# Filler transposes kept to the first part, later landing estimates, and two tiles' diagonals moved to ScalarE

## Chip, cores and metric

One core of one Trainium2 chip. The metric is device time in microseconds for one launch. TensorE (PE), VectorE (DVE), ScalarE (ACT), GpSimd (POOL) and SyncE (SP) each run their own instruction stream in order; streams meet only through semaphores.

## The reference

Three stages follow one another on 3072 tokens (batch 4, sequence 768, 8 heads of 48):

```
for t in range(S):                      # attention: linear recurrence per batch and head
    cur = outer(u * k[t], v[t])
    y[t] = r[t] @ (state + cur)
    state = w * state + outer(k[t], v[t])
x  = y as 3072 x 384
h  = x @ w_in                           # 384 -> 2048
x2 = (h * sigmoid(h)) @ w_out           # 2048 -> 384
e  = argmax(x2 @ w_gate + bias[modality])       # one of 8 experts
out[token] = gate * (relu(x2[token] @ w1[e]) @ w2[e])   # 384 -> 1024 -> 384
```

## The kernel before

**Attention** is done in 24 chunks ("tiles") of 128 tokens, `attention(n)`. A tile's inputs come by two DMAs: `load_A` (r and k transposed, and v: 768 KB) and `load_B` (r and k as rows: 192 KB, or 384 KB from tile 9 on, `NZ = 9`). Three buffers (two `AB` and `stall`) take turns from tile 3 on. Then r and k are scaled by powers of w (L460 on DVE, L464 on POOL, L462 for the first three tiles), the scores are formed on PE (L487) and put by `copy_predicated` (L493, DVE) over a matrix whose diagonal holds the u term. That diagonal matrix is ident times a column, formed by ScalarE in eight `activation` calls (L475), except for the tiles in `DIAG_POOL = (1, 2)`, where GpSimd does it in two `tensor_tensor` calls (L469). PE then multiplies by v and by the state (L503), the result is split in two parts (L524, L527), and the state is updated (L544, L557, L559, L548).

**The first dense layer** runs over 8 blocks of 384 tokens and 16 slices of its hidden width (`moe1`): nine matmuls into `ph` (L618), SiLU and a split into a high and a low part (L622, L623, L625), nine matmuls into `pa` (L637). The weights of the 16 slices are loaded (L290) and split first (`convert`, L587 to L596). Blocks 0 and 1 are done in two halves; the second half is added to the first by DVE (L653). `route` follows a block: transposes (L686), logits (L697, L702), expert choice, and writing of the rows to DRAM (L764).

**The experts** are `expert(s)`, s from 0 to 8: gathers of rows (L915), weight splitting (L925, L929), matmuls (L949, L957), scaling (L961, L963) and scatter to the output (L966). Steps 0 to 7 take 384 tokens each, step 8 takes 128. A loop for tokens left over follows (L1078); each engine reads its count first (L1077), and all engines meet there.

**Order of the work.** All of this is first put into a list of operations, each with an engine, an estimated duration, a priority, dependencies and buffers to acquire and release. `Plan.order` runs these through a small event simulation in Python when the kernel is built: at each moment each engine takes the ready operation of the lowest priority number whose buffers are free. The start times that come out fix the order in which instructions are emitted. The plan's clock is not used on the chip; only the order stays. For an operation with `nbytes` the plan lets the bytes pass at 260 KB per us after those of earlier transfers, and adds 4.0 us until what depends on it may start. A load of tile n is ready for the plan when a buffer is free; the conditional DMA of L425 (it moves data only in a fallback for extreme decay rates) stands behind it on SP and waits for its landing.

**Fillers.** A hundred operations of priority 900 and up, each of four transposes of `ident` whose result nobody reads, acquire an `h` or an `a` bank. They come last in priority, so the plan places one wherever PE would have nothing else to do, at 0.45 us each:

```
    for i in range(100):
        add("PE", 0.45, 900 + i, lambda i=i: [pe.transpose(bank(("w", i))[:, 0:128], ident, ident) for _ in range(4)],
            acq=[("ha"[i % 2], ("w", i))], rel=[("w", i)], lat=0.0)
```

Fifty more such transposes (L305) stand at the very start, outside the plan.

Of the kernel before, what the change touches and what calls it, by code (L numbers as in the profile page):

```python
# [16 lines left out]
SP = mybir.EngineType.SP  # L17
# [21 lines left out]
VW = 128  # L39
AW = 8 * C + 4 * VW  # L40
TW = AW + 2 * DM
DIAG_POOL = (1, 2)
NZ = 9
ENGINES = ("PE", "ACT", "DVE", "POOL", "SP")
HALF = NFC // 2
# [11 lines left out]
class Plan:  # L57
# [7 lines left out]
    def add(self, eng, dur, prio, fn, deps=(), acq=(), rel=(), lat=0.2, nbytes=0):  # L65
        o = Op()
        o.eng, o.dur, o.prio, o.fn, o.lat, o.nbytes = eng, dur, prio, fn, lat, nbytes
        o.deps = [d for d in deps if d is not None]
        o.acq, o.rel = list(acq), list(rel)
        o.n, o.after, o.left = len(self.ops), [], 0  # L70
        self.ops.append(o)
        return o

    def order(self):
        for o in self.ops:
            o.left = len(o.deps)
            for d in o.deps:
                d.after.append(o)
        ready = {e: [] for e in ENGINES}
        busy = dict.fromkeys(ENGINES, 0.0)  # L80
        events, dma, t, done = [], 0.0, 0.0, []
        for o in self.ops:
            if not o.left:
                heapq.heappush(ready[o.eng], (o.prio, o.n, o))
        count = 0
        while True:
            moved = True
            while moved:
                moved = False
                for e in ENGINES:  # L90
                    if busy[e] > t + 1e-9 or not ready[e]:
                        continue
                    held, pick = [], None
                    while ready[e]:
                        x = heapq.heappop(ready[e])
                        need = {}
                        for p, _ in x[2].acq:
                            need[p] = need.get(p, 0) + 1
                        if all(len(self.free[p]) >= k for p, k in need.items()):
                            pick = x[2]  # L100
                            break
                        held.append(x)
                    for x in held:
                        heapq.heappush(ready[e], x)
                    if pick is None:
                        continue
                    o = pick
                    for p, key in o.acq:
                        self.slot[key] = (p, self.free[p].pop(0))
                    o.start = t  # L110
                    busy[e] = t + o.dur
                    end = t + o.dur + o.lat
                    if o.nbytes:
                        dma = max(dma, t + o.dur) + o.nbytes / 260e3
                        end = dma + 4.0
                    heapq.heappush(events, (busy[e], count, None))
                    heapq.heappush(events, (end, count + 1, o))
                    count += 2
                    done.append(o)
                    moved = True  # L120
            if not events:
                break
            t = events[0][0]
            while events and events[0][0] <= t + 1e-9:
                o = heapq.heappop(events)[2]
                if o is None:
                    continue
                for key in o.rel:
                    p, i = self.slot[key]
                    self.free[p].append(i)  # L130
                for a in o.after:
                    a.left -= 1
                    if not a.left:
                        heapq.heappush(ready[a.eng], (a.prio, a.n, a))
        assert len(done) == len(self.ops), (len(done), len(self.ops))
        self.span = t
        return sorted(done, key=lambda o: (o.start, o.n))


def moe_rwkv_kernel(tc, ins, out):  # L140
# [51 lines left out]
    tA = [t[:, 0:8 * C].rearrange("p (a q t) -> p a q t", a=2, q=4) for t in AB]  # L192
# [90 lines left out]
    def load_A(n, s):  # L283
        sp.dma_start(AB[s][:, 0:AW], ins["av"][n])

    def load_B(n, s, w_=0):
        sp.dma_start(AB[s][:, AW + w_ * DM:], ins["rk"][n * C:(n + 1) * C, w_ * DM:])
# [52 lines left out]
    for i in range(NP):  # L340
        n = 1 << i
# [12 lines left out]
    add = P.add  # L354
# [4 lines left out]
    def sl_(key):  # L359
        return P.slot[key][1]  # L360
# [5 lines left out]
    def gate(t):  # L366
        return add("POOL", 0.0, -99, lambda: None, lat=t)
# [3 lines left out]
# [3 lines that stand above are left out]
# [22 lines left out]
    def need_at(n):  # L396
        j, i = divmod(n, BT)
        gap = {0: 1.0, 1: 2.6, 2: 2.6}.get(j, NFC / BT)
        return FIRST[j] - 0.4 - (BT - 1 - i) * gap
# [8 lines left out]
    def attention(n):  # L408
        b, c = n % B, n // B
        j, i = divmod(n, BT)  # L410
        z = need_at(n)
        pp = ("tah", "htt", "att")[n] if n < 3 else "ttt"
        kA, kT = ("A", n), ("atb", n)
        if n < 3:
            P.slot[kA] = ("tA", n)
            if n < 2:
                P.free["tA"].remove(n)
            oA, oB = gate((0.1, 0.2, 2.2)[n]), add("SP", 0.5, -49 + n, lambda: load_B(n, n, 1), nbytes=200e3)
        else:
            oA = add("SP", 0.6, z - 9, lambda: load_A(n, sl_(kA)), acq=[("tA", kA)], nbytes=786e3)  # L420
            oB = add("SP", 0.6, z - 8.9, lambda: load_B(n, sl_(kA), int(n < NZ)), [oA], nbytes=393e3 if n >= NZ else 197e3)
        relA = [kA] if n != 2 else []

        def f_V():
# [40 lines left out]
        o_d = []  # L465
        if n in DIAG_POOL:
            for hf in range(2):
# [597 lines left out]
    for n in range(NTILE):  # L1065
        j = n // BT
        if n % BT == 0 and j >= 2:
            run_moe(max(i for i, x in enumerate(SEQ) if x[0] == j - 2) + 1)
        attention(n)
# [3 lines left out]
        expert(s)  # L1073
    with tc.manual_schedule():
        for o in P.order():
            o.fn()
    tn = nc.values_load(tailn, min_val=0, max_val=NMAX - NSTAT + NA + 1)  # L1077
    with tc.For_i(0, tn, 1) as i:  # L1078
        e_ids("t", lists[1], bass.ds(i + (NSTAT - 1 - NA), 1))
# [91 lines left out]
```

## Time and profile before

| | us |
|---|---|
| median of 3 runs | 808.32 (807.42 to 811.14) |
| the profiled execution | 806.15 |
| its span, first to last instruction | 804.4 |

The mean granted TensorE clock of the profiled execution is 0.995 of full speed. A view of the profile names instructions by engine and line; PE is the matmul itself, PEld the load of its weights, and an engine's name with a q its sequencer. Times are us from the start of the span unless marked ns.

### The profile page before, as it was taken

The page shows a single profiled execution, that of the slowest core. Times are in us where ns is not written, and L with a number is a line of the kernel's source. Part 1 is how long each engine was busy: PE and PEld are TensorE (multiplying, and loading weights), DVE is VectorE, ACT ScalarE, POOL GpSimd, SP SyncE. Part 2 cuts the span into 40 slices and gives each one's busy share as a digit, 9 for nine tenths or more (in the row PEclk, how much of TensorE's full clock was granted, in tenths as well). Part 3 has the DMA queues.
Part 4 walks back from the last instruction along what each step waited for, and adds up shares of the span by engine and source line. Part 5 has one row for each costly group of instructions (what it writes and reads, how often), then busy time and mean ns, then how long its engine had stood idle before and what let it go on. Part 6 is the DMA issues. An engine that isn't in the chain of part 4 may idle for free.

```text
span 804.4 us, 15749 instructions
## 1 busy us (share of the span) xinstructions
PE 791.2 (98%) x6348; PEld 760.0 (94%) x6348; DVE 425.7 (53%) x793; ACT 337.3 (42%) x726; POOL 227.9 (28%) x280
## 2 busy tenths in 40 slices
PE   8999999998999999999999999999999999999998
PEld 7998999987999999999999999999999999999998
DVE  7989965635534543644643522353866544654310
ACT  3566765443334334334334422364435434444200
POOL 5435302343423422522421203210432313220120
PEclk9999999998999999999999999999999999999999
DMA  6454433081511411411421024531675345500000
GB/s 245 153 177 184 167 119 108 28 79 44 90 59 59 91 60 60 89 60 61 85 65 59 11 22 180 224 120 68 217 217 187 128 135 199 196 28 1 30 35 2
DMA packets 23920, 83.27 MB, mean 104 GB/s; under 512 B 7659, under 2 KB 12152, under 8 KB 21538
## 3 DMA queue, kind: packets, MB, share of 16 engines
q1 hardware_dynamic: 19730, 72.55, 30.1%
q0 software_dynamic: 3968, 9.66, 3.6%
q8 instruction: 51, 0.84, 0.5%
q14 instruction: 27, 0.22, 0.2%
q10 hardware_dynamic: 144, 0.00, 0.0%
HBM read 78.92 MB, written 9.77 MB: 110 GB/s over the span
## 4 chain that ended last, share of the span: by engine, by line
PE 90%; DVE 4%; DMA 3%; issue 1%; ACT 1%; POOL 1%; DVEq 0%; POOLq 0%; SPq 0%; ACTq 0%
PE ph L618 24%; PE pa L637 23%; PE ph L949 13%; PE pa L957 12%; PE pt L503 4%; PE pa L372 3%; PE pt L487 3%; PE ph L372 2%; DMA xgb<-x_rows,it 2%; DMA AB<-in_av_dram 1%; PE pt L933 1%; PE ph L305 1%; PE pt L686 1%; PE pt L544 1%; PE pt L697 1%
## 5 line engine op out<-in xcount | busy, mean ns | idle before, releaser
L625 DVE TENSOR_TENSOR gl<-sg,gh 128x384 fp32r<-128x384 f32 x128 | 86.7, 677 | 136.4 <-ACT gh L623 135.9
L622 ACT ACTIVATE sg<-ph 128x384 f32<-128x384 f32 x128 | 63.0, 492 | 214.0 <-PE ph L618 205.6
L637 PE MATMUL pa<-Wh,gh 128*128 128x384 f32 x384 | 132.7, 346 | 0.0
L637 PE MATMUL pa<-Wh,gl 128*128 128x384 f32 x384 | 129.7, 338 | 0.5 <-DVE gl L625 0.4
L637 PE MATMUL pa<-Wl,gh 128*128 128x384 f32 x384 | 128.8, 335 | 0.0
L618 PE MATMUL ph<-xh,Wh 128*128 128x384 f32 x384 | 92.8, 349 | 0.0
L618 PE MATMUL ph<-xh,Wl 128*128 128x384 f32 x384 | 88.9, 339 | 0.1
L618 PE MATMUL ph<-xl,Wh 128*128 128x384 f32 x384 | 88.5, 338 | 0.0
L1034 ACT ACTIVATE gh<-ph 128x384 fp32r<-128x384 f32 (+1 forms) x66 | 32.7, 495 | 113.5 <-PE ph L949 112.9
L1036 DVE SCALAR_TENSOR_TENSOR gl<-ph,gh 128x384 fp32r<-128x384 f32 (+1 forms) x66 | 36.8, 558 | 81.1 <-ACT gh L1034 81.1
L637 PEld LDWEIGHTS pa<-Wh,gh 128*128 128x128 f32 x384 | 72.3, 188 | 3.2 <-issue 2.0
L637 PEld LDWEIGHTS pa<-Wh,gl 128*128 128x128 f32 x384 | 72.1, 188 | 1.2 <-DVE gl L625 1.2
L637 PEld LDWEIGHTS pa<-Wl,gh 128*128 128x128 f32 x384 | 72.3, 188 | 0.0
L618 PEld LDWEIGHTS ph<-xh,Wh 128*128 128x128 f32 x384 | 66.3, 189 | 4.8 <-issue 3.2
L966 POOL DMA_INDIRECT out_dram<-x2all,it x25 | 33.8, 1353 | 127.8 <-DVE x2all L963 114.6
L618 PEld LDWEIGHTS ph<-xh,Wl 128*128 128x128 f32 x384 | 69.3, 188 | 0.7 <-DVE Wl L596 0.7
L618 PEld LDWEIGHTS ph<-xl,Wh 128*128 128x128 f32 x384 | 69.5, 189 | 0.0
L929 DVE TENSOR_TENSOR Wl<-raw,Wh 128x1024 fp32r<-128x1024 f32 (+2 forms) x54 | 64.0, 1220 | 9.9 <-ACT Wh L925 9.9
L957 PE MATMUL pa<-Wh,gh 128*128 128x384 f32 x200 | 67.6, 338 | 0.8 <-DVE x2all L963 0.8
L957 PE MATMUL pa<-Wh,gl 128*128 128x384 f32 x200 | 67.5, 337 | 0.0
L957 PE MATMUL pa<-Wl,gh 128*128 128x384 f32 x200 | 67.0, 335 | 0.0
L475 ACT ACTIVATE atall<-ident,cs 128x128 f32<-128x128 f32 x176 | 57.2, 393 | 13.8 <-DVE cs L457 9.8
(226 smaller groups left out, 1385.2 us busy)
## 6 DMA issues: line engine op xcount, KB each, us to landing
raw<-in_we_dram SPq DMA_DIRECT2D x18, 1536.0 KB
AB<-in_av_dram SPq DMA_DIRECT2D x18, 768.0 KB
stall<-in_wio_dram SPq DMA_DIRECT2D x16, 768.0 KB
x_rows<-x2all SPq DMA_DIRECT2D x24, 192.5 KB
AB<-y_slow SPq DMA_DIRECT2D x16, 256.0 KB
stall<-in_av_dram SPq DMA_DIRECT2D x5, 768.0 KB
AB<-in_rk_dram SPq DMA_DIRECT2D x10, 384.0 KB
stall<-in_rk_dram SPq DMA_DIRECT2D x5, 384.0 KB
```

What stands on the lines that cost most here:

```text
L372: add("PE", 0.45, 900 + i, lambda i=i: [pe.transpose(bank(("w", i))[:, 0:128], ident, ident) for _ in range(4)], acq=[("ha"[i % 2], ("w", ...
L475: act.activation(atb[sl_(kT)][h % 2][:, h // 2, :], ident, AF.Copy, scale=cs[:, h:h + 1])
L618: pe.matmul(p, win(a, fc, kt), (xh, xl)[b_][j % 2][:, kt, :], start=i == 0, stop=i == len(ops) - 1)
L622: o_s = add("ACT", 0.5, s - 4, lambda: act.activation(sgb[sl_(kS)], hps[sl_(kH)][:, 0:n], AF.Silu), [o_g1], acq=[("sg", kS)])
L625: o_l = add("DVE", 0.55, s - 4, lambda: vv.tensor_tensor(glb[sl_(kG)][:, 0:n], sgb[sl_(kS)], ghb[sl_(kG)][:, 0:n].bitcast(F32), op=ALU.sub ...
L637: pe.matmul(a, g[:, ts], wout(wp_, fc), start=begin and i == 0, stop=end and i == 2)
L929: eng.tensor_tensor(e_view(buf, 1)[wi][sl], m2[s]["raw", wi][sl], e_view(buf, 0)[wi][sl].bitcast(F32), op=ALU.subtract)
L949: pe.matmul(p[:, i * n:(i + 1) * n], a[:, kt, fc * 128:(fc + 1) * 128], b_[xb][:, kt, 0:n], start=m == 0, stop=m == len(ops) - 1)
L957: pe.matmul(a[:, 0:DM], g[:, sl], wt_[:, fc, :], start=fc == 0 and m == 0, stop=fc == NFE - 1 and m == 2)
L966: i = gp.indirect_dma_start(out=out, out_offset=bass.IndirectOffsetOnAxis(ap=m2[s]["it"][:, t:t + 1], axis=0), in_=o, in_offset=None, boun ...
L1034: o2 = add("ACT", 0.62 if small else 0.5, z + k - 6, lambda kH=kH, kG=kG, m=m: act.activation(ghb[sl_(kG)][:, 0:m], hps[sl_(kH)][:, 0:m], ...
L1036: o3 = add("DVE", 0.7 if small else 0.57, z + k - 6, lambda kH=kH, kG=kG, m=m: vv.scalar_tensor_tensor(glb[sl_(kG)][:, 0:m], hps[sl_(kH)][ ...
```

## The change

Three edits. Fillers whose start on the plan's clock is 150 or later are not emitted (the plan still places them). For the loads of tiles 9 to 23 the plan expects the landing 7.8 us later (`load_A`) and 5.8 us later (`load_B`) than before; for every other transfer, 3.8 plus the default `lat` of 0.2 is the 4.0 of before. And no tile has its diagonal formed by GpSimd any more.

```diff
-DIAG_POOL = (1, 2)
+DIAG_POOL = ()
@@ Plan.order
                     if o.nbytes:
                         dma = max(dma, t + o.dur) + o.nbytes / 260e3
-                        end = dma + 4.0
+                        end = dma + 3.8 + o.lat
@@ attention
-            oA = add("SP", 0.6, z - 9, lambda: load_A(n, sl_(kA)), acq=[("tA", kA)], nbytes=786e3)
-            oB = add("SP", 0.6, z - 8.9, lambda: load_B(n, sl_(kA), int(n < NZ)), [oA], nbytes=393e3 if n >= NZ else 197e3)
+            oA = add("SP", 0.6, z - 9, lambda: load_A(n, sl_(kA)), acq=[("tA", kA)], nbytes=786e3, lat=8.0 if n >= NZ else 0.2)
+            oB = add("SP", 0.6, z - 8.9, lambda: load_B(n, sl_(kA), int(n < NZ)), [oA], nbytes=393e3 if n >= NZ else 197e3, lat=6.0 if n >= NZ else 0.2)
@@ the emission
         for o in P.order():
-            o.fn()
+            if o.prio < 900 or o.start < 150.0:
+                o.fn()
```

## Rows read from the trace of the kernel before

**Rows 1.** The page, part 1: busy time, share of span, instructions.
```profile
PE 791.2 (98%) x6348; PEld 760.0 (94%) x6348; DVE 425.7 (53%) x793; ACT 337.3 (42%) x726; POOL 227.9 (28%) x280
```

**Rows 2.** Busy time by stage, the filler line L372 alone (x is its count).
```profile
0.00:134.00 134.00, 23.35 (x180) 20.06 (x180) 1.00 0.46 163
134.00:772.50 638.50, 0.00 (x0) 0.00 (x0) 0.99 0.33 95
772.50:801.20 28.70, 24.50 (x220) 24.20 (x220) 1.00 0.07 24
```

**Rows 3.** The chain that ended last, 755 to 805: start, us, what.
```profile
772.96 1.31 PE ph L372 x12
...
776.36 0.44 PE pa L372 x4
776.79 2.09 PE pa L957 x12
778.89 8.30 PE pa L372 x76
```

**Rows 4.** Timeline at the end: start, us, engine, line, [idle before <-releaser].
```profile
772.47 0.58 ACT L961 ACTIVATE x2all<-pa,gt 128x384 f32<-128x384 f32 x1 [0.49 <-PE pa L957]
...
772.62 1.14 DVE L963 TENSOR_SCALAR x2all<-pa,gt 128x384 f32<-128x384 f32 x2
```

**Rows 5.** Line L1078 by engine: ns min/median/max, first and last start.
```profile
L1078 SPq EVENT_SEMAPHORE  x16: 17/28/16415, 696.4 to 799.6; - x16
...
L1078 PEldq EVENT_SEMAPHORE  x13: 51/51/51, 801.2 to 803.0; - x13
```

**Rows 6.** The chain that ended last, 130 to 200.
```profile
144.79 0.66 PE pt L686 x6
...
170.07 0.49 PE pt L544 x16
...
173.97 9.30 DMA AB<-in_av_dram
...
184.02 0.57 DVE x2all L653
...
184.63 1.54 PE pt L686 x6
186.18 2.88 PE ph L618 x9
```

**Rows 7.** Timeline of all engines, 183 to 185.
```profile
183.29 0.69 DVE L460 TENSOR_TENSOR AB<-AB,Pt 128x512 f32<-128x512 f32 x1 [6.72 <-DMA AB<-in_av_dram]
...
184.63 0.69 PE L686 MATMUL pt<-ident,x2all 128*128 128x128 f32 x2 [4.44 <-DVE x2all L653]
```

**Rows 8.** Busy us by 20 us: PE, PEld, DVE, ACT, POOL; clock, DMA.
```profile
180.00:200.00 20.00, 15.56 (x151) 14.05 (x151) 10.88 (x27) 6.59 (x18) 6.59 (x8) 0.83 0.11 45
...
500.00:520.00 20.00, 19.24 (x127) 18.41 (x126) 6.85 (x30) 7.35 (x19) 2.89 (x8) 1.00 0.69 281
```

**Rows 9.** Line L487 from 160 to 270: ns, first and last start.
```profile
L487 PE MATMUL pt<-stall x32: 272/272/373, 191.2 to 254.3; 48*128 48x128 f32 x32
```

**Rows 10.** SP's queue, 60 to 330: what waits for tile 12's landing.
```profile
204.95 0.09 SPq L425 DMA_DIRECT2D stall<-y_slow  x1
```

**Rows 11.** Timeline of ACT, POOL and DVE, 11 to 50.
```profile
13.58 2.45 ACT L475 ACTIVATE atall<-ident,cs 128x128 f32<-128x128 f32 x8 [4.47 <-DVE cs L457]
...
23.01 2.76 POOL L469 TENSOR_TENSOR atall<-ident,cs 128x512 f32<-128x512 f32 x2 [3.27 <-DVE cs L457]
...
17.04 1.79 DVE L592 SCALAR_TENSOR_TENSOR cx<-cx,stall 128x768 uint32<-128x768 uint32 x1
...
38.12 0.96 DVE L592 SCALAR_TENSOR_TENSOR cx<-cx,stall 128x768 uint32<-128x768 uint32 x1
```

**Rows 12.** The chain that ended last, 0 to 60.
```profile
31.78 0.44 PE ph L372 x4
32.21 1.60 PE ph L618 x9
```

## The prediction

> **What bounds the kernel now.** I read the page first: PE is busy for 791.2 of 804.4 us [rows 1], so the span is PE's instruction stream, and the question is only which part of that stream is work and where it still stands idle. The second view is the busy time of the filler line alone, by stage [rows 2]. The reader should see three numbers there: 180 transposes up to 134 us, none for the next 638 us, and 220 after 772.5 us. The fillers of the middle do not exist, because the plan found PE full there; those that were left over were placed at the end of the plan, after everything else. The third view is the chain at the end [rows 3] with the timeline of the other engines [rows 4]: the last real matmuls end at 778.9 us, and what the chain shows behind them is filler. The fourth, the semaphores of the closing loop [rows 5], shows what that costs: SP stood 16.4 us at one semaphore that ended at 799.6, while PE's own semaphores of that line begin at 801.2. So the other engines were through at about 783.2 and the span waited for fillers.
>
> The fifth view is the chain around 180 us [rows 6] and its timeline [rows 7], because a table by 20 us showed one stage where PE was busy for only 15.56 us, with a granted clock of 0.83 [rows 8]. There PE waited 4.44 us for DVE's L653, and DVE had stood 6.72 us in front of L460, the scaling of tile 11 (numbers of tiles follow from the order of the 24 loads), whose load landed only at 183.27 [rows 6]. L653 has nothing to do with tile 11; it stood behind L460 in DVE's stream.
>
> **The fillers at the end.** The edit removes those that the plan starts at 150 or later. The plan's clock and the chip's differ, but between the two groups lies an empty 638 us [rows 2], so a threshold anywhere in it removes the 220 and keeps the 180. What PE's end sets after that: the engines meet at 783.2 instead of 799.6, which is 16.4 us. To this comes what the fillers between the last real matmuls cost: 1.31 us at 772.96 and 0.44 us at 776.36 [rows 3]. The second comes back whole. The first only in part, since the matmuls behind it need an accumulator that ACT and DVE were emptying: ACT's scaling ends at 773.05, DVE's two at 773.76 [rows 4]. The fillers ended at 774.27, so 0.5 to 1.2 us come back. I take 0.8, as the plan gives out the bank that came free first, less a little for the hand-over. Together 1.2 us, bounds 0.9 and 1.6. Last, what follows the meeting: it took 4.8 us (799.6 to 804.4), but PE's semaphores of L1078 began only at 801.2, when its fillers were through, so up to 1.6 us of this belong to the fillers too; the rest may be PE's own branch. Half of it is 0.8. Sum: 16.4 + 1.2 + 0.8 = 18.4 us, bounds 17.3 (16.4 + 0.9) and 19.6 (16.4 + 1.6 + 1.6).
>
> Without fillers PE stands idle for up to a us at 773. A pause of 0.76 us in the stage from 500 to 520 left the clock at 1.00, and the pause of 4.44 us was the one after which it fell [rows 7, 8]; the new pause is nearest to the short one, so I cost it at nothing. The Trainium skill, "TensorE: Matmul & The Clock Gate", section "HAM oscillation — how this bites in real kernels", speaks against taking fillers away: a PE that pauses between bursts of matmuls goes back to the lower clock. By it the end would be as under "clock" below; the two pauses of this trace leave that a small chance.
>
> **Landings expected later.** This edit adds no instruction and no transfer; it moves places in the streams. For tile 11 the plan's clock starts where the last reader of the buffer, L544, ends: 170.07 + 0.49 = 170.56 [rows 6]. Before, it expected the landing 0.6 + 786/260 + 4.0 = 7.6 us later, that is at 178.2; the real one came 12.7 us later, since SP issued the load only at 173.97 and it then took 9.30 us. DVE was there at 183.29 - 6.72 = 176.6 and stood. With the edit the plan expects 15.4 us, or 186.0, which is later than the real landing. L653's input came from matmuls that ended before 180.19 (184.63 - 4.44, where PE ran dry), so in the plan L653 goes ahead of L460, and PE goes on at once. What comes back: 4.44 us of idle time, and the lower clock after it. L618's nine matmuls took 2.88 us there [rows 6] and 1.60 elsewhere [rows 12], six transposes 1.54 instead of 0.66 [rows 6]: 2.2 us. Sum 6.6 us. If another stall takes its place, or this one stays, nothing: the bounds are 0 and 6.6.
>
> What is moved behind each load is L460 on DVE, L464 and the products of r, k and u on POOL, and L425 on SP, which waits for the landing. SP and POOL gain: what stands behind these in their streams, the row stores of L764 and the state scaling of L548, no longer waits for a load. None of the moved work is close to its need: tile 12 had landed at 204.95 [rows 10], and its scores are the last of the L487 row, at 253 to 254 [rows 9]. 7.8 us out of 48 are hidden by that distance.
>
> **The diagonals of tiles 1 and 2.** Four GpSimd instructions go, 16 ScalarE instructions come. One tile's eight took 2.45 us on ScalarE, GpSimd's pair 2.76 [rows 11], so the step itself shortens by 0.3 us for a tile; but the first of the two mask copies needed only GpSimd's first half, and now needs seven of eight activations. Behind the 16 on ScalarE stand L587 and L595 of the weight conversion and L524 of the tile before. From above: if all of it falls on the path to the first dense matmuls, 2 x 2.45 = 4.9 us slower. From below: DVE gets faster, because L592 took 1.79 us beside GpSimd's pair and 0.96 without [rows 11]; three such instructions at 0.83 give 2.5 us. The first real L618 came right behind fillers [rows 12], so in this stage PE's stream does not wait for DVE; the plan's own gaps, filled, set the time. DVE's relief does not enter the plan, and on the plan's clock eight activations cost 2.56 us against 2.8 for the pair. I take 0.
>
> The Trainium skill, "GPSIMD Engine Reference", section "8. Key points", says that GpSimd shares its SBUF interfaces with VectorE and that the two contend when VectorE reads two SBUF inputs. L592 has two such inputs, and the trace agrees (1.79 against 0.96 us). By that rule alone the first part would shorten; it is the "relief" below.
>
> **Sum.** 18.4 + 6.6 + 0 = 25.0 us. Against the profiled execution: span 804.4 - 25.0 = 779.4, its own time 806.15 - 25.0 = 781.2. The median of the runs shown lies 2.2 us above that execution, so 808.3 - 25.0 = 783.3, which I predict.
>
> **Rivals.** *Stall stays or moves*, 0.18: the plan's new order puts another DVE instruction in front of PE's next input, or tile 11's load is later still because more stores now go ahead of it on SP. For it: the real lag of 12.7 us is only 2.7 below the new estimate. Against it: with DVE moved, only a load later by that much does harm. 808.3 - 18.4 = 789.9. *ScalarE late*, 0.10: the 16 activations hold up conversion; PE's count of fillers before 134 us would grow. 783.3 + 4.9 = 788.2. *Relief*, 0.08: 783.3 - 2.5 = 780.8. *Clock*, 0.04: the pause at 773 lets the clock fall for the last two groups of matmuls, which took 2.09 us each [rows 3]; 783.3 + 4.2 = 787.5. *Starved*, slower than before, 0.02: the later landings push a tile's scores past their need, and PE, whose gaps no longer get fillers after 150, stands idle. There are 15 such tiles; up to 7.8 us each would give 783.3 + 117 = 900, and it outweighs the gain from 1.7 us a tile (25.0 / 15). It decides only if the distance of 48 us is used up, which nothing in the rows does. My forecast has 0.58.
>
> **How the numbers follow.** Low end: the upper bound of the end (1.2 more) and relief (2.5 more) give 779.6; the profiled execution's place under the median takes 2.1 off that, 777.5. High end: the stall case, 789.9, with a little of the lower bound of the end, 790.5. Relief, ScalarE and clock lie within. A difference of 0.5% (4 us) is about what a measurement of this kernel can tell from none. All cases but the last are faster by far more; for several small losses together I leave 0.02 within 0.5%. So faster 0.96, same 0.02, slower 0.02.
>
> **What would show it.** The filler line has about 180 transposes, all before some 140 us, and none at the end; the engines meet within 2 us of the last scatter's landing. No stage after 20 us has a clock under 1.00, and DVE's L460 has no long wait for a DMA. L475 counts 192, L469 is gone, L592 has no 1.79 any more, and the first L618 of the chain stands within 2 us of 32.2. The prediction is wrong if the clock falls in some stage between 140 and 770, if the count of early fillers changes by more than 20 transposes, or if the meeting at the end waits for something other than PE.

## The result, and the profile after

The changed kernel took 781.89 us (median of four runs, 780.16 to 783.08) against 809.73 for the kernel before in the same rounds; the ratio is 0.9652, with a 95% interval from 0.961 to 0.9693. The forecast was 783.3 in a range from 777.5 to 790.5. The profiled execution's span fell from 804.4 to 778.4 us, by 26.0 where the sum said 25.0; the two medians lie 27.8 us apart. One execution of the changed kernel in a later round (e11) took 1912.51 us, for a reason that no trace here shows, and is left out of every median and ratio below.

To see where it went I cut both spans at the same pieces of PE's work: the first dense matmul (L618), the first transposes of `route` (L686), the matmuls of tile 9 (the tenth group of L503, as tiles count from 0), and the last expert matmul (L957). These times are the starts of PE's instructions in the traces, the last one an end. The third row holds the stall at 180 us. The first two rows do not hold the same work on both sides, as shown under "The first part".

| us | before | after | difference |
|---|---|---|---|
| start to the first L618 | 32.0 | 33.1 | +1.1 |
| to the first L686 | 110.8 | 110.7 | -0.1 |
| to tile 9's L503 | 52.2 | 45.3 | -6.9 |
| to the end of the last L957 | 584.0 | 582.0 | -2.0 |
| to the end of the span | 25.5 | 7.4 | -18.1 |

**The end.** PE has 28 us less to do than in [rows 1], and the filler line has no instruction after 140 us, where [rows 2] had 220. The page's first part, then the filler line by stage (PE, PEld, clock, DMA):

```profile
PE 763.3 (98%) x6104; PEld 733.9 (94%) x6104; DVE 400.1 (51%) x793; ACT 341.8 (44%) x742; POOL 214.1 (28%) x276
```

```profile
0.00:140.00 140.00, 19.52 (x156) 17.36 (x156) 0.98 0.47 164
140.00:770.00 630.00, 0.00 (x0) 0.00 (x0) 1.00 0.30 95
770.00:778.00 8.00, 0.00 (x0) 0.00 (x0) 0.88 0.15 52
```

The closing loop's semaphores answer to [rows 5] (the line is now L1079). Under them stand SP's waits that end in the last 18 us (us in total, times, longest); the longest began far ahead of that window:

```profile
L1079 SPq EVENT_SEMAPHORE  x16: 17/28/892, 690.0 to 775.1; - x16
...
L1079 PEldq EVENT_SEMAPHORE  x13: 51/51/1100, 771.1 to 775.5; - x13
```

```profile
SPq L1079 <- DMA out_dram<-x2all,it: 83.8, 2, 82.9
```

PE's first semaphore of that line now begins at 771.1, right behind its last matmul, and SP's last one at 775.1. What SP waits for is the last scatter's landing and no longer PE. From the meeting to the end of the span it is 3.3 us (775.1 to 778.4), where it was 4.8.

**The stage at 180.** Busy time by stretch (PE, PEld, DVE, ACT, POOL, clock, DMA), for [rows 8] and two more; then PE's and DVE's timeline, for [rows 6, 7]:

```profile
40.00:60.00 20.00, 18.02 (x151) 16.85 (x151) 13.96 (x19) 12.12 (x29) 3.62 (x3) 0.83 0.35 122
180.00:200.00 20.00, 20.00 (x200) 18.38 (x199) 12.01 (x34) 8.33 (x23) 8.81 (x12) 1.00 0.39 120
...
766.00:771.00 5.00, 4.85 (x27) 4.28 (x25) 1.28 (x3) 0.58 (x1) 3.15 (x6) 1.00 0.21 79
```

```profile
180.51 0.69 PE L618 MATMUL ph<-xl,Wh 128*128 128x384 f32 x3
181.04 0.90 PE L686 MATMUL pt<-ident,x2all 128*128 128x128 f32 x6
```

```profile
180.32 1.49 DVE L653 TENSOR_TENSOR x2all<-pa,x2all 128x384 f32<-128x384 f32 x3
...
187.81 1.21 DVE L460 TENSOR_TENSOR AB<-AB,Pt 128x512 f32<-128x512 f32 x1
```

L653 now stands ahead of tile 11's L460, PE has no idle time in the stage, and its clock is 1.00.

**The first part.** PE's order changed here. The state matmuls (L544) of three tiles stood behind the first L618 before (first fence) and stand ahead of it now (second fence), with four transposes more; behind the first L618 there are 60 transposes of L372 instead of 88. PE is busy for 28.76 us up to the first L618 before and for 29.84 after, and idle for 3.2 us in both.

```profile
31.97 0.78 PE L618 MATMUL ph<-xh,Wh 128*128 128x384 f32 x3
...
33.74 0.56 PE L544 MATMUL ph<-AB 128*48 128x48 f32 x16
```

```profile
28.98 0.56 PE L544 MATMUL ph<-AB 128*48 128x48 f32 x16
...
30.88 0.53 PE L544 MATMUL pt<-x2all 128*48 128x48 f32 x16
...
33.06 0.78 PE L618 MATMUL ph<-xh,Wh 128*128 128x384 f32 x3
```

The row from 40 to 60 is new: 18.02 us busy, clock 0.83, where the kernel before has 19.92 and 1.00. PE's timeline shows a pause of 1.56 us, and six us from 46 on at 0.50 of full speed, which is 1.2 GHz (the window stands under it):

```profile
41.22 0.95 PE L454 MATMUL pt<-ub,zb 128*128 128x2 f32 x8
43.73 1.16 PE L487 MATMUL pt<-AB 48*128 48x128 f32 x16 [1.56 <-issue]
```

```profile
46.00:52.00 6.00, 6.00 (x21) 6.00 (x21) 3.27 (x6) 4.36 (x11) 1.00 (x1) 0.50 0.02 7
```

DVE and GpSimd at the same time, for [rows 11]:

```profile
16.74 0.95 DVE L592 SCALAR_TENSOR_TENSOR cx<-cx,stall 128x768 uint32<-128x768 uint32 x1
...
36.30 1.92 DVE L592 SCALAR_TENSOR_TENSOR cx<-cx,stall 128x768 uint32<-128x768 uint32 x1
38.14 1.64 DVE L625 TENSOR_TENSOR gl<-sg,gh 128x384 fp32r<-128x384 f32 x1
39.70 2.05 DVE L594 CUSTOM_DVE_ANT_0 cx<-stall,cx 128x1536 uint16<-128x1536 uint16 x1
...
42.95 0.68 DVE L460 TENSOR_TENSOR AB<-AB,Pt 128x512 f32<-128x512 f32 x1
```

```profile
35.92 1.48 POOL L464 TENSOR_TENSOR AB<-AB,Qt 128x512 f32<-128x512 f32 x1
...
39.44 1.50 POOL L464 TENSOR_TENSOR AB<-AB,Qt 128x512 f32<-128x512 f32 x1
40.90 1.71 POOL L480 TENSOR_TENSOR AB<-AB,PKt 128x384 f32<-128x384 f32 x1
```

Tile 3's L460 ends at 43.63, and PE goes on with tile 3's scores (L487) at 43.73. L592 took 0.95 us where GpSimd's diagonals had stood beside it (16.74), but 1.92 beside GpSimd's scaling of tiles 3 and 4. ScalarE has the 16 added activations, 192 in all:

```profile
L475 ACT ACTIVATE atall<-ident,cs 128x128 f32<-128x128 f32 x192 | 62.0, 397 | 18.9 <-DVE cs L457 10.5 <-DMA x2all<-y_slow 4.3 <-DVE cs L440 3.9
```

### The profile page after: what moved, and what is told of

Read it like the earlier page. It is cut to its first block, busy times and chain, and to the rows that moved or that the text cites. A ratio compares the mean times of both kernels' runs of the same rounds, so it can differ in the third digit from the quotient of the medians.

```text
span 778.4 us, 15275 instructions
## 1 busy us (share of the span) xinstructions
PE 763.3 (98%) x6104; PEld 733.9 (94%) x6104; DVE 400.1 (51%) x793; ACT 341.8 (44%) x742; POOL 214.1 (28%) x276
## 5 line engine op out<-in xcount | busy, mean ns | idle before, releaser
L625 DVE TENSOR_TENSOR gl<-sg,gh 128x384 fp32r<-128x384 f32 x128 | 81.0, 633 | 154.5 <-ACT gh L623 146.6
L618 PE MATMUL ph<-xh,Wh 128*128 128x384 f32 x384 | 92.9, 350 | 0.0
L618 PE MATMUL ph<-xh,Wl 128*128 128x384 f32 x384 | 88.8, 339 | 0.0
L618 PE MATMUL ph<-xl,Wh 128*128 128x384 f32 x384 | 88.5, 338 | 0.0
L618 PEld LDWEIGHTS ph<-xh,Wh 128*128 128x128 f32 x384 | 66.2, 189 | 4.4 <-issue 3.0
L475 ACT ACTIVATE atall<-ident,cs 128x128 f32<-128x128 f32 x192 | 62.0, 397 | 18.9 <-DVE cs L457 10.5
L618 PEld LDWEIGHTS ph<-xl,Wh 128*128 128x128 f32 x384 | 69.5, 189 | 0.0
L618 PEld LDWEIGHTS ph<-xh,Wl 128*128 128x128 f32 x384 | 69.5, 188 | 0.0
L957 PE MATMUL pa<-Wh,gh 128*128 128x384 f32 x200 | 67.5, 337 | 1.0 <-DVE x2all L963 0.8
L957 PE MATMUL pa<-Wh,gl 128*128 128x384 f32 x200 | 67.4, 337 | 0.0
L957 PE MATMUL pa<-Wl,gh 128*128 128x384 f32 x200 | 67.0, 335 | 0.0
```

The source lines that it names most:

```text
L475: act.activation(atb[sl_(kT)][h % 2][:, h // 2, :], ident, AF.Copy, scale=cs[:, h:h + 1])
L618: pe.matmul(p, win(a, fc, kt), (xh, xl)[b_][j % 2][:, kt, :], start=i == 0, stop=i == len(ops) - 1)
L625: o_l = add("DVE", 0.55, s - 4, lambda: vv.tensor_tensor(glb[sl_(kG)][:, 0:n], sgb[sl_(kS)], ghb[sl_(kG)][:, 0:n].bitcast(F32), op=ALU.sub ...
L957: pe.matmul(a[:, 0:DM], g[:, sl], wt_[:, fc, :], start=fc == 0 and m == 0, stop=fc == NFE - 1 and m == 2)
```

## The experiments

There were twelve runs. The cuts of the table above, for the profiled execution of each:

| kernel | to first L618 | to first L686 | to tile 9's L503 | to last L957 | to end | span |
|---|---|---|---|---|---|---|
| before | 32.0 | 110.8 | 52.2 | 584.0 | 25.5 | 804.4 |
| after | 33.1 | 110.7 | 45.3 | 582.0 | 7.4 | 778.4 |
| after, again (e11) | 33.4 | 109.1 | 47.0 | 581.8 | 7.7 | 778.9 |
| e1, fillers alone | 31.3 | 110.9 | 52.2 | 582.6 | 7.4 | 784.3 |
| e2, landings alone | 31.0 | 111.2 | 48.5 | 586.2 | 25.5 | 802.5 |
| e3, diagonals alone | 33.3 | 108.7 | 51.0 | 585.3 | 28.1 | 806.4 |
| e4, e1 with e2 | 31.1 | 110.5 | 47.2 | 585.0 | 7.5 | 781.3 |
| e5, landing of tile 11 alone | 34.8 | 111.1 | 45.4 | 584.2 | 25.5 | 800.9 |
| e6, after with a bridge | 33.1 | 107.4 | 45.3 | 582.0 | 7.3 | 775.2 |
| the bridge again (e12) | 32.5 | 107.4 | 49.2 | 583.3 | 7.3 | 779.7 |
| e7, after with no filler | 32.4 | 114.2 | 45.4 | 584.1 | 7.3 | 783.5 |
| e8, e4 with 3 for 4 | 30.9 | 110.1 | 45.3 | 582.4 | 7.4 | 776.1 |
| e9, after, GpSimd relieved | 36.6 | 105.9 | 47.7 | 583.8 | 7.7 | 781.6 |
| e10, e6 with 3 for 4 | 34.1 | 108.6 | 47.3 | 583.1 | 7.7 | 780.9 |

### Fillers alone (e1)

```diff
         for o in P.order():
-            o.fn()
+            if o.prio < 900 or o.start < 150.0:
+                o.fn()
```

> Only the fillers after 150 are left out; landings and diagonals as in the kernel before. Theory (the end waits for PE alone): the streams are the same up to 772 us, so the span falls by what the two ends differ in, 19.5 us (1.3 between the last matmuls, 18.2 behind them), to about 785; PE's 4.44 us stall and the lower clock between 180 and 190 stay. Rival (the other engines' own closing work sets the end and only part comes back): 12 us or less.

Median 789.97, ratio 0.9769 (0.9729 to 0.9808), span 784.3, 20.1 us shorter. Behind the last L957 it is 7.4 us instead of 25.5, and tile 9 to the last L957 is 1.4 shorter. The stall at 180 is untouched:

```profile
184.83 1.54 PE L686 MATMUL pt<-ident,x2all 128*128 128x128 f32 x6 [4.43 <-DVE x2all L653]
```

### Landings alone (e2), and that of tile 11 alone (e5)

```diff
-                        end = dma + 4.0
+                        end = dma + 3.8 + o.lat
```

with `lat=8.0` and `6.0` for tiles 9 to 23 in e2, and for `n == 11` alone in e5.

> Only the landing estimates are changed; all 400 fillers and GpSimd's diagonals stay. Theory (one DVE instruction in front of another block's drain): the first 140 us are as before, the stall at 180 us goes with the lower clock after it, span shorter by 6.9 us, to about 797.5, with 220 fillers at the end. Rival (a stall moves elsewhere, the gain seen in the full change comes from its other first part): span within 2 us of before.

Median 804.72, ratio 0.994 (0.9905 to 0.9975), span 802.5: 1.9 us shorter, where 6.9 was expected (by the ratio, over ten executions, it is 4.9 us). The stall is gone, but the stage has a new pause, and another stands at 405, both in the middle of a group of matmuls that waits for no semaphore:

```profile
178.36 0.69 PE L618 MATMUL ph<-xh,Wl 128*128 128x384 f32 x3 [2.91 <-issue]
...
406.90 0.57 PE L503 MATMUL pt<-atall,AB 128*32 128x128 f32 x5 [1.69 <-issue]
```

> The kernel before with the later landing for tile 11 alone (all 220 late fillers stay). Theory: the landing term is one load's. The stall of 4.42 to 4.44 us at 180 and the low clock behind it go, the stage from the first L686 to tile 9's L503 shortens by 3.7 (as in the run with all landings) to 6.9 us (as in the changed kernel), and the span goes from 804.4 to 797.5 to 800.7. Rival: the later landings of the other 14 tiles carry part of it, then the stage shortens by less than 2 us. Second rival: the order shifts where PE's code comes in, and a pause in the middle of a group of matmuls takes 1.5 to 3 us of it back at some other place.

Median 799.77, ratio 0.9898 (0.9847 to 0.9949). The stage takes 45.4 us instead of 52.2: the whole gain, from one load. Its span shows only 3.5 of it, since this execution came to its first L618 2.8 us later than the one of before, with the same instructions up to there: the clock was 0.50 from 16 to 22 us, where before has 1.00, and PE had not been idle from 10 to 15.5 us. DVE's timeline, the stage and that stretch:

```profile
180.80 1.60 DVE L653 TENSOR_TENSOR x2all<-pa,x2all 128x384 f32<-128x384 f32 x3 [1.54 <-PE pa L637]
...
188.32 0.69 DVE L460 TENSOR_TENSOR AB<-AB,Pt 128x512 f32<-128x512 f32 x1
```

```profile
180.00:200.00 20.00, 20.00 (x201) 18.45 (x200) 10.80 (x32) 7.95 (x21) 3.46 (x7) 1.00 0.37 87
...
16.00:22.00 6.00, 6.00 (x41) 5.22 (x42) 6.00 (x9) 1.07 (x2) 3.14 (x2) 0.50 0.55 172
```

So the term is tile 11's alone; the later landings of the other 14 tiles brought nothing that shows.

### Diagonals alone (e3), and the other two edits without them (e4)

```diff
-DIAG_POOL = (1, 2)
+DIAG_POOL = ()
```

> Only the diagonals of tiles 1 and 2 go to ScalarE. Theory (this edit alone changes the first part): 156 fillers before 134 us, a pause of 1.5 to 2 us near 43 us with a lower clock to about 52 us, and the first transposes of L686 about 1 us later than before; span 1 us longer at that place (804 to 807 in all, as the stall at 180 us may shift). Rival (the first part's change comes from the landing estimates): 180 fillers, nothing at 43 us.

Median 809.08, ratio 1.0011 (0.998 to 1.0042): no difference. The table shows what cancels. The first L618 comes 1.3 us later, behind the three L544 and the four transposes more that the changed kernel has there too. The plan finds 24 fewer places for early transposes in all (156 instead of 180, as after the change), 28 fewer of them behind the first L618, and the stretch up to the first L686 is 2.1 us shorter. In this kernel the 24 reappear at the end, which is 2.6 us longer (28.1 against 25.5). The stage at 180 is 1.2 us shorter and what follows 1.3 longer. The pause at 43 is here too, with the clock at 0.91 from 40 to 60, so it belongs to this edit:

```profile
43.58 1.16 PE L487 MATMUL pt<-AB 48*128 48x128 f32 x16 [1.19 <-POOL AB L480]
```

> The full change without its diagonals: GpSimd keeps tiles 1 and 2. Theory (the diagonals cost 1.0 us net): span about 777.4, 1 us shorter than with the full change, 180 early fillers, no lower clock between 40 and 60 us. Rival (ScalarE's diagonals pay): span above 779.

Median 783.53, ratio 0.9694 (0.9626 to 0.9763), span 781.3. The gains of e1 and of the stall add up, less two pauses at the places of e2:

```profile
176.37 0.68 PE L618 MATMUL ph<-xh,Wl 128*128 128x384 f32 x3 [1.56 <-issue]
...
404.90 0.52 PE L503 MATMUL pt<-atall,AB 128*32 128x128 f32 x6 [1.68 <-issue]
```

Since the whole change has neither pause, it looked at this point as if the diagonals' edit paid 2.9 us by shifting PE's code. The next runs were to test that.

### PE's code shifted (e8)

```diff
-        ... lambda i=i: [pe.transpose(bank(("w", i))[:, 0:128], ident, ident) for _ in range(4)],
+        ... lambda i=i: [pe.transpose(bank(("w", i))[:, 0:128], ident, ident) for _ in range(3)],
```

> Fillers and landings edited, diagonals as before (profiled span 781.3), with three transposes for each early filler in place of four. PE's instruction stream gets some 90 instructions shorter ahead of 140 us, so that the 16 KB pieces of its code (256 instructions) are fetched some 8 us later against the work around them. Theory (the pauses of 1.56 us at 174.8 and 1.67 us at 403.2 come from a slow fetch of PE's code behind tile's index lists' small scatters): both pauses go or move to another group, the stage from the first L686 to tile 9's L503 is 1.5 us shorter (45.7 instead of 47.2), and the span 777 to 780 if the first part stays. Rival (the pauses belong to these groups of matmuls, whatever the fetch): both stay at the same groups and the span changes by less than 1 us. The first part shows besides whether a filler costs PE time: up to 4.9 us earlier if so, 0 if not.

Median 779.44, ratio 0.9654 (0.9611 to 0.9697), span 776.1. Both pauses were gone and the stage took 45.3 us, as the theory said; fillers a quarter shorter gave 0.4 us in the first part. But the fetch that the theory blames was there as before. Of q8, which fetches one 16 KB packet of code at a time, here is the one packet in e2 from 169 to 176 us, and in e8 from 163 to 170; 3.1 and 3.2% of 16 engines over 7 us are 3.5 and 3.6 us, where most such packets took 0.9 to 1.3. Only e2 paused behind it:

```profile
q8 instruction: 1, 0.02, 3.1%
```

```profile
q8 instruction: 1, 0.02, 3.2%
```

### The bridge (e6), the control (e11) and the bridge again (e12)

```diff
         def f_sc(qs):
+            if n == 3:
+                for _ in range(14):
+                    pe.transpose(bank(("sc", n, 0))[:, 0:128], ident, ident)
             for q in qs:
```

> The changed kernel with 14 more transposes into the score bank right ahead of tile 3's scores, where PE paused for 1.56 us at 42.2 to 43.7 and after which the granted clock was 0.50 from about 45 to 52.5. Theory: the pause is what let the clock fall. With it bridged the window from 40 to 60 has a clock of 0.97 or more instead of 0.83, the first L686 comes 2 to 3.5 us earlier (140.3 to 141.8 instead of 143.75), and the span is 775 to 776.5 instead of 778.4. Rival: the clock fell for another reason, such as the narrow matmuls ahead of the pause; then the low stretch stays and the span is 778.4 to 780.

Median 777.54, ratio 0.9638 (0.9599 to 0.9677), span 775.2. The stretch to the first L686 is 3.3 us shorter than after, and the clock in the window is 1.00, with the eight narrow matmuls (L454) still there. (Lines behind L482 count three more here: L485 is the bridge, L490 the scores.)

```profile
41.29 0.95 PE L454 MATMUL pt<-ub,zb 128*128 128x2 f32 x8
42.10 1.73 PE L485 MATMUL pt<-ident 128*128 128x128 f32 x14
43.76 0.49 PE L490 MATMUL pt<-AB 48*128 48x128 f32 x4
```

```profile
40.00:60.00 20.00, 19.64 (x190) 18.36 (x189) 16.64 (x24) 14.75 (x34) 4.06 (x3) 1.00 0.47 157
```

Three us lie within the intervals of runs made apart, so the changed kernel and the bridge ran once more in the same rounds.

> The changed kernel itself once more, as a control on the same chip and in the same rounds as the kernel with the bridge, since 3 us lie within the intervals of runs made apart. Theory: PE's pause ahead of tile 3's scores belongs to this instruction stream and comes again (1 to 1.6 us near 42), with a granted clock under 0.95 in 40 to 60; the span is 778 to 781. Rival: it was an accident of one execution, then the clock there is 1.00 and the span 775 to 776.5.

Ratio 0.9685 (0.9657 to 0.9712), median 781.27, span 778.9. The pause is back at the same scores, the clock of the window is 0.91:

```profile
44.03 1.16 PE L487 MATMUL pt<-AB 48*128 48x128 f32 x16 [1.57 <-POOL AB L480]
```

> The changed kernel with the bridge once more, beside the control. Theory: no pause near 42, clock 0.97 or more in 40 to 60, and a median 2 to 3.5 us under that of the control in the same rounds. Rival: the 3.2 us between the two profiled spans were scatter from one execution to the next; then the two medians differ by less than 1 us.

Ratio 0.9674 (0.9644 to 0.9704), median 781.14. At its place the bridge did what it did before: no pause near 42, clock 1.00, and a stretch of 107.4 us, as in e6. But the median is only 0.1 us under the control's, so the rival's number came out, though the mean clock of an execution is 0.994 to 0.998 here and 0.990 to 0.994 in the control. What takes the clock's gain back can be seen in the one profiled execution alone. The profiled span is 779.7, 4.5 us above that of the very same kernel in e6, because two pauses now stand where e2 and e4 had them, the first with a clock of 0.50 behind it (178 to 180.5):

```profile
40.00:60.00 20.00, 19.63 (x190) 18.35 (x189) 16.61 (x25) 15.42 (x34) 2.97 (x3) 1.00 0.48 169
```

```profile
176.17 0.42 PE L621 MATMUL ph<-xl,Wh 128*128 128x384 f32 x1 [2.08 <-issue]
...
405.31 0.33 PE L640 MATMUL pa<-Wl,gh 128*128 128x384 f32 x1 [1.33 <-issue]
```

This takes the shifted code down as an explanation: one instruction stream has the pauses in one execution and not in the other. Nor is a slow fetch needed, as the first of the two shows. Around the pause at 174 to 176 the queues of this execution moved only a tile's loads from 172.5 to 176.2, and q8's one packet from 161 to 175 took 0.4% of 16 engines over 14 us, or 0.9 us:

```profile
q8 instruction: 1, 0.02, 0.4%
```

### No fillers at all (e7)

```diff
-            if o.prio < 900 or o.start < 150.0:
+            if o.prio < 900:
```

> The changed kernel with the 156 early transposes of L372 left out too. Theory A (they fill gaps that PE has anyway and hold the clock): without them the first part has stages at the granted clock of 0.50 and lower means, the first L686 comes at 146 or later instead of 143.75, and the span is 781 to 790. Theory B (they stand in PE's way): each four take 0.45 us or less of PE's time, 156 of them at most 17 us, the clock stays at 1.00 in most stages, and the span is 765 to 777.

Median 781.92, ratio 0.9673 (0.962 to 0.9727), span 783.5. Theory A: the stretch to the first L686 is 3.5 us longer, with pauses of 3.04 us at 25 and 1.60 at 43, and the clock well down:

```profile
20.00:40.00 20.00, 15.30 (x161) 12.36 (x153) 17.52 (x20) 14.54 (x31) 8.37 (x6) 0.68 0.63 208
40.00:60.00 20.00, 17.98 (x141) 16.82 (x142) 14.44 (x20) 11.10 (x25) 4.16 (x3) 0.74 0.29 97
```

The early fillers' 19.5 us of PE time cost nothing that shows and hold the clock, but what they hold is worth some 3 us of one span, and the ratio cannot tell it from the changed kernel's.

### GpSimd relieved (e9)

```diff
-            o_k = add("POOL", 1.4, z - 3.2, lambda: gp.tensor_tensor(*scale(1), op=ALU.mult), zd)
+            o_k = add("POOL", 1.4, z - 3.2, lambda: gp.tensor_tensor(*[x[:, 0:1] if n in (3, 4) else x for x in scale(1)], op=ALU.mult), zd)
```

and the same cut for `nat(1), nat(1), PKt` of these two tiles.

> The changed kernel, same order on every engine, but GpSimd's scaling of k for tiles 3 and 4 (two L464 of 128x512) and its product for the state there (two L480 of 128x384) work on a part only (128x128 and 128x48), so the output of these tiles lacks the rest. Theory: DVE is slow between 34.5 and 43 us because GpSimd works beside it (L592 1.92 us instead of 0.96, L594 2.05 instead of 0.96), and that makes PE pause at 42.2. With some 4 us less of GpSimd's work there, DVE reaches tile 3's L460 by 41.5 or earlier instead of 42.95, PE's pause of 1.5 us goes or falls under 0.5, the clock in 40 to 60 is 0.97 or more, and the span is 775 to 776.5, as with the bridge. Rival: DVE is late for its own amount of work; then L592 and L594 there may be quicker, but the pause stays over 1 us and the span stays within 1 us of the changed kernel's.

Median 776.22, ratio 0.9616 (0.9589 to 0.9643), which is 0.69% or 5.6 us under the control in the same rounds by the ratios (5.1 by the medians), and the intervals do not touch. DVE's timeline:

```profile
38.75 1.94 DVE L592 SCALAR_TENSOR_TENSOR cx<-cx,stall 128x768 uint32<-128x768 uint32 x1
40.61 0.82 DVE L625 TENSOR_TENSOR gl<-sg,gh 128x384 fp32r<-128x384 f32 x1
41.35 0.94 DVE L594 CUSTOM_DVE_ANT_0 cx<-stall,cx 128x1536 uint16<-128x1536 uint16 x1
...
43.78 0.95 DVE L460 TENSOR_TENSOR AB<-AB,Pt 128x512 f32<-128x512 f32 x1
```

This execution came to its first L618 3.5 us late, again with a clock of 0.50 from 16 to 22; counted from there, tile 3's L460 begins 7.2 us on, and 9.9 us after the change (42.95 - 33.06). DVE was as late as PE (L590 at 38.15 and at 34.64 after the change), so its gain is not the late start's. L594 took 0.94 us instead of 2.05, while L592, at 1.94, gained nothing. PE has no pause near 43, and the stretch to the first L686 is the shortest of all, 105.9 us. The expected span of 775 to 776.5 did not come (781.6): the late start, and pauses of 0.41 and 1.17 us near 179 and 1.43 at 407, took it back in this execution, while its other runs took 775.2 to 778.3 us. The first part explains 3.2 to 4.8 us (109.1 and 110.7 against 105.9) of the 5.6; the rest is not placed. This kernel's output is another one, so the choice of experts may differ too; no run separates that.

### The bridge with shorter fillers (e10)

The bridge of e6 with three transposes for four.

> The changed kernel with the 14 transposes of the bridge and three transposes for each early filler in place of four (117 in place of 156 if the plan keeps its count). Theory: fillers fill gaps, so a quarter fewer give back 0.5 us at most, as between the two runs without the diagonals' edit (first L686 at 141.05 with three, 141.55 with four), and may cost as much where the clock falls in the first 20 us: span 774 to 776.5 against 775.2. Rival: PE's code shifts and a pause in the middle of a group of matmuls shows up between 150 and 500; then 776.5 to 779.

Median 778.93, ratio 0.9636 (0.9609 to 0.9663), span 780.9: above both expected ranges, and the longest of its five executions (the others 774.5 to 777.3). A new pause of 0.88 us stands at 41, a clock of 0.88 and 0.95 in the first two stretches of 20 us, a late start (34.1), and 1.70 us at 180. No kernel with all its work can be told from the changed one by more than its interval.

## Why the prediction was right, and where it was not

**Fillers at the end: 18.4, measured 19.5.** The sum lay inside its bounds (17.3 to 19.6): 16.7 up to the meeting (20.7 us behind the last matmul before, 4.0 after; I had 16.4), 1.3 between the last two groups of matmuls (7.5 from the last L949 to the last L957 before, 6.2 after; 1.2), and 1.5 behind the meeting (4.8 to 3.3; 0.8). The part that was mis-sized is the last: I gave PE's own branch half of 1.6 us, and nearly all of it belonged to the fillers. The clock did not fall there: 1.00 from 766 to 771, PE busy for 4.85 of 5 us. (The 0.76 us between 500 and 520 by which I priced it were not one pause but two waits of 0.38 us, in front of L739 and L740.) On one point the prediction contradicts itself: it says that the engines meet at the last scatter's landing, which they do, and also that a meeting that waits for something other than PE would make it wrong.

**Landings: 6.6, measured 6.9.** The order of L653 and L460, the idle time and the clock came out as worked out. That one load carries it was implied and is shown by e5 (6.8 us in the stage). In e2 and e4 only 3.7 and 5.0 us of it can be seen in the stage; what lies between is pauses of 2.9 and 1.6 us that also come in kernels where nothing of this edit differs (e12 against e6). The rival that the stall moves did not come true: DVE's L460 has no wait for a DMA left that holds anything up.

**Diagonals: 0, measured 0, but by another way.** The step "in this stage PE's stream does not wait for DVE; the plan's own gaps, filled, set the time" failed. The plan lost 24 of its early transposes, more than the 20 that I had set as a bound, and found PE full where the chip's PE then stood for 1.56 us for DVE's L460. The first L618 comes 0.5 to 2.4 us later (32.5 to 33.4 in after, e3, e6, e11 and e12, against 31.0 to 32.0 in before, e1, e2 and e4; e5, e9 and e10 had a low clock ahead of it). PE is not idle for longer up to there than before (3.2 us). What stands ahead of L618 in addition is 3 x 0.49 for L544 [rows 6] and 0.44 for four transposes [rows 12], 1.9 us: the order of PE's work, so that no run shows the ScalarE rival. Behind the first L618 PE is then spared those 1.5 us of L544 and the 3.1 us of 28 transposes at 0.11 us [rows 12], and pays 2.1 to 2.4 us more idle time (3.1 in after and e11, 2.8 in e3, against 0.7) and, as an estimate, 1.8 to 3.4 us for the low clock (0.91 and 0.83 over 20 us). These terms would leave the stretch between 0.7 us shorter (e3) and 1.2 us longer (after); it is 0.1 to 2.1 us shorter, so that some 1.3 us are not placed. That does not make a transpose fewer worth its time: e8, with 45 fewer, gained 0.4 us. The first L686 comes at 143.75, 142.45 and 141.98 with the edit (after, e11, e3), and at 142.73, 142.14, 142.20 and 141.55 without (before, e1, e2, e4). e3 confirms the 0 end to end: 1.0011, with 24 more transposes at its end in it. That gains and losses come to nothing here is luck: no step of the prediction has them.

**"No stage after 20 us with a clock under 1.00" was wrong.** I priced a pause only at the end, by the two pauses in [rows 7, 8], and looked at none that the new order of the first part could open. Behind one of 1.56 us the clock was 0.50 from 46 to 52. Both executions of the changed kernel have the pause and the low clock, both of the bridge have neither. In the cuts this is worth 1.7 to 3.3 us (109.1 and 110.7 against 107.4), in the medians of e11 and e12 nothing that shows. The Trainium skill's "TensorE: Matmul & The Clock Gate", section "HAM oscillation — how this bites in real kernels", which I had weighed for the wrong place, says that a PE that pauses between bursts goes back to the lower clock. Behind this pause the trace agrees (0.50), behind the 2.91 us of e2 it does not (1.00 from 175 to 185); at the end, where I quoted it, no run shows a fall ahead of PE's last matmul.

**What makes DVE late there** is in part GpSimd beside it: with two of GpSimd's instructions cut to a quarter and two to an eighth, and every order kept, L594 goes from 2.05 to 0.94 us and the pause is gone (e9). The kernel before has an L594 of 2.05 us too (at 40.58) and no pause, because its PE came to tile 3's scores only at 46.29, when L460 had ended (44.41 + 1.78); so the earlier place that the plan gave those scores is as much part of the cause. The Trainium skill's "GPSIMD Engine Reference", section "8. Key points", says that the two share SBUF interfaces and contend where VectorE reads two SBUF inputs; the trace agrees for L592, 1.92 us beside GpSimd and 0.95 without. The relief that I had taken from it for tiles 1 and 2 did come (0.95 instead of 1.79 at 16.74); 20 us later L592 took 1.92 us beside GpSimd.

**The total** was closer than its parts: +1.1 at the end, +0.3 at the stall, +0.6 between tile 9 and the last L949, and -1.0 in the first part make the 26.0 from the 25.0. Two of the signs that were to show the prediction wrong came out: the count of early transposes (24 fewer), which belongs to the step that failed, and the meeting, which now waits for the last scatter's landing, as the working had it.

**What stays open** is what holds PE in the middle of a group near 175 and 404 us. It comes in some executions and not in others of one kernel, so no edit here is needed for it. A slow fetch of code stands ahead of it in e2 and e4 and ahead of the one at 404 in e12 (3.0 us, between 399 and 405), but not ahead of the one at 175 in e12, and e8 has the slow fetch without a pause. Open as well is why the clock fell at 16 us in e5 and e9.

## What to carry to other kernels

Work that a scheduler places to keep an engine busy is free only as long as real work follows on that engine; behind the last of it, it is the critical path, so look first at what the engines wait for where they meet. A wrong estimate in a plan costs where an instruction that waits stands ahead of one that the bottleneck needs, so ask of each load what is queued behind its first reader, and expect the gain from that one place. A profiled span is one execution: two of the same kernel differed by 4.5 us here, so cut the span at common pieces of work, and run the unchanged kernel in the same rounds, before an edit is given credit for three.

## What the runs showed of the hardware that was not expected

- Pauses of PE in the middle of a group of matmuls, with no open semaphore in the profile: 1.3 to 2.9 us, in e2, e4 and e12 near 175 and 404 us, none in before, after and e6. They alone are worth some half a per cent of the span in e2 (4.6 us).
- The first L618 came 30.9 to 36.6 us after the start over all kernels, and at 31.0 (e2) and 34.8 (e5) behind the same instructions. The clock makes the difference: 1.00 from 16 to 22 us in e2, 0.50 in e5, with PE busy for 5.39 and 5.50 of the 5.5 us from 10 to 15.5. So the clock fell in e5 with no pause just ahead of it.
- Nor does the length of a pause alone tell what the clock does. It fell to 0.50 after 1.56 us at 43 in the changed kernel, ahead of which PE had run eight matmuls of two columns in 0.95 us, and after 2.08 us at 175 in e12; it stayed at 1.00 after 1.15 us at 76 in the changed kernel and after 2.91 us at 177 in e2.
- A GpSimd multiplication cut to a quarter (128x128 instead of 128x512) took 0.66 to 1.06 us (e9) instead of 1.48 to 1.88 (after and e11).
